# Building the token lists of a routed layer: number columns as 32-wide weights in four column groups, the one-hot table streamed, one small product to sum and turn

## The chip, the cores and the metric

The kernel runs on one core of one Trainium2 chip. The metric is the device time of one execution in microseconds (us), as the median of several runs; less is better. The core's engines are TensorE (PE; its weight loads are shown apart as PEld), VectorE (DVE), ScalarE (ACT), GpSimd (POOL), and SyncE (SP), which issues most DMAs. Each engine runs its own instructions strictly in the order in which the program gave them to it, and waits for the others by semaphores.

## The reference

Retention (attention with a decaying mask and no softmax) over 8 batches and 8 heads gives 4608 tokens of 512 numbers. They go through a layer of 8 experts with a fixed capacity of 576 tokens each, and through a dense two-layer network.

```python
scores = scale * np.matmul(q, k.transpose(0, 1, 3, 2))
ret = scores * Dmat[None, :, :, :]
x = np.matmul(ret, v)                       # 4608 x 512 after a reshape

logits = x @ w_gate                         # 4608 x 8
order = np.argsort(-logits.flatten())
for idx in order:                           # the greedy choice, with capacity 576
    tok, e = (int(idx) // E, int(idx) % E)
    if assigned[tok] >= 0 or counts[e] >= cap:
        continue
    assigned[tok] = e
    counts[e] += 1
for e in range(E):
    mask = assigned == e
    h = np.maximum(x[mask] @ w1[e], 0.0)
    out[mask] = h @ w2[e]

h = np.maximum(x @ w_in, 0.0)
return (h * h @ w_out).astype(np.float32)
```

## The kernel before

**Stages.** Attention runs for the first 169 us over 36 tiles of 128 tokens. Then `turn_back` writes the tokens to a DRAM table `xd` (36 groups of four PE transposes), while the router works out which 576 tokens the first expert gets. From about 218 us on, `moe(k)` for the experts k = 0 to 7 alternates with `mlp(j)`, the dense network on three tiles of 128 rows: one block after an even k, two after an odd k. An expert is two parts of 8 chunks f: a group of 12 products from `XH`, `XL` (the expert's tokens, turned) into a tile `mm` (L802), and, two chunks later, a group of 12 into the four `acc` tiles (L785). An `mlp` block is 16 chunks of a group of 12 (L865) and three groups of 9 (L849; one for each of its tiles).

**Weights.** `pump` moves the weight stream on: it splits one fetched chunk `raw` (two buffers, 512 KB) into a high and a low half `w` (ACT twice L628, POOL L629, DVE L630), and has SP fetch the next one into the buffer that came free. A chunk is split at most three ahead of use.

**Routing.** `Router.phase(k)` is a generator: it finds the threshold of expert k by binary search (`G`, `dg`, `cc`, `cx`, `cf`, `jk`; products L421 and L431), and then lists its tokens. At each `yield` it gives control back, and `slot()`, called twice in each chunk, moves it on by one step every few calls. `slot()` also moves on `load_tokens`, which waits until `listed(k)` has been called, issues the gathers of the expert's rows (POOL, L708, by the numbers in `idx`), and then `turn`s them: four PE transposes into `mm` (L716), ACT's copy `XH` (L724), DVE's difference `XL` (L725). When a part of `moe(k)` begins, `turned(n)` runs router and loader without pause until as many turns as the part needs (3, then 5) have been emitted.

**The list** of expert k (L498 to L518). DVE makes a one-hot table `OH` of 12 tokens tiles at a time, [128, 128, 12] f16 with the tile index t innermost, so that the 128 columns of one t lie 24 bytes apart. For each of 36 t, the PE loads the 128x128 slice `oh[:, :, t]` as weights and streams ten columns of `HC` (five of the token's tile number x 128, five of its row): all add into one `p[:, :10]`, which holds the numbers of the listed tokens already turned, one list entry to a partition. DVE copies `ids`, adds the two halves and writes `idx` as integers.

**The first expert's start** (L887 to L899): a loop moves the router and `turn_back` on and calls `pump` in each pass until the first list is done; then come 36 `warm` transposes, the loader until three turns are out, and one more `pump`.

Of the kernel before, what the change touches and what calls it, by code (L numbers as in the profile page):

```python
# [6 lines left out]
F32 = mybir.dt.float32  # L7
# [3 lines left out]
FH = mybir.dt.float16  # L11
# [4 lines left out]
NT = 36  # L16
# [53 lines left out]
def attention(tc, a, X, idn, rt, filler):  # L70

    nc = tc.nc
    L = rt.L
    with ExitStack() as c:
        cn = c.enter_context(tc.tile_pool(name="acn", bufs=1))
# [4 lines left out]
        def load(t, w0=0, w1=3):  # L80

            src = a["att"][t].rearrange("p (w g i) -> p w g i", w=3, g=4)
            if w0 == 0:
                T[t] = wk.tile([128, 2, 4, 128], F32, name="qk", bufs=5)
                nc.sync.dma_start(T[t], src[:, :2])
            if w1 == 3:
                V[t] = wk.tile([128, 4, 128], F32, name="v", bufs=4)
                nc.sync.dma_start(V[t], src[:, 2])
# [16 lines left out]
        wg = cn.tile([128, 4, 32], F32, name="wg")  # L105
        nc.vector.memset(wg, 0.0)
        nc.sync.dma_start(wg[:, :, :NE], a["wg"])
        nc.sync.dma_start(rt.f, a["rt"])
        load(3, 0, 2)
        load(2, 2, 3)  # L110
        load(4, 0, 2)
# [111 lines left out]
        for t in range(NT):  # L223
            if t + 2 < NT:
                turn_k(t + 2)
            if t + 1 < NT:
                weigh(t + 1)
                scores(t + 1)
            if t + 5 < NT:
                load(t + 5, 0, 2)  # L230
            if t + 3 < NT:
                load(t + 3, 2, 3)
            if t + 2 < 9:
                decay(t + 2)
            before(t)
            if t >= 4 and t % 2 == 0:
                next(todo, None)
            values(t)
            if t % 9 != 8:
                state(t)  # L240
            if t == NT - 2:
                ready = rt.prep(0, 32)
            if t >= NT - 2:
                next(ready)
            if t == 3:
                rt.start()
            next(filler, None)
        last = [gate(32, 35), gate(35, 36, "sp")]
        for g in last:
# [7 lines left out]
def route_tables():  # L257
    i = np.arange(128)
    tri = (i[:, None] < i[None, :]).astype(np.float32)
    u = np.zeros((128, 72), np.float32)  # L260
    j = np.arange(72)
    u[:72] = j[:, None] < j[None, :]
    thr = np.zeros((4, 16), np.float32)
    off = 0
    for r, step in enumerate(STEPS):
        thr[r] = np.arange(16) * step - off
        off += step
    sel = np.zeros((128, 4, 8), np.float32)
    for tl in range(4):
        sel[tl * 8:tl * 8 + 8, tl] = np.eye(8)  # L270
    f = np.concatenate([np.tile(thr.reshape(1, 64), (128, 1)),
                        np.tile(8.0 - np.arange(8), (128, 1)),
                        np.tile(128.0 * np.arange(36), (128, 1)),
                        i[:, None].astype(np.float32),
                        np.zeros((128, 8)),
                        np.tile(np.arange(8.0), (128, 1)),
                        np.tile(i, (128, 1)),
                        tri, u,
                        i[:, None] // 16 == np.arange(8),
                        i[:, None] % 16 == np.arange(16),  # L280
                        np.where(i < 8, CAP, BIG)[:, None],
                        sel.reshape(128, 32),
                        ], axis=1)
    return np.ascontiguousarray(f, np.float32)


# [6 lines left out]
class Router:  # L293
# [6 lines left out]
    def __init__(self, tc, pool):  # L300
        self.nc, self.ps = tc.nc, None
        t = pool.tile
        self.L = t([128, NT, 8], F32, name="L")
        f = self.f = t([128, 510], F32, name="rt")
        self.thr = f[:, 0:64].rearrange("p (r j) -> p r j", r=4)
        self.w8 = f[:, 64:72]
        self.t128 = f[:, 72:108]
        self.pcol = f[:, 108:109]
        self.e8 = f[:, 117:125]
        self.m8, self.m16 = f[:, 453:461], f[:, 461:477]  # L310
        self.c8 = f[:, 477:478]
        self.io = t([128, 128, 12], FH, name="io")
        self.b = t([128, 128 + 72], FH, name="rtb")
        self.tri, self.u = self.b[:, 0:128], self.b[:, 128:200]
        self.OH = [t([128, 128, 12], FH, name=f"OH{i}") for i in range(2)]
        self.sel = self.OH[0].rearrange("p s t -> p (s t)")[:, :512].rearrange("p (t m) -> p t m", t=4)
        self.ones = t([128, 128], FH, name="ones")
        self.U = t([128, NT], F32, name="U")
        self.AS = t([128, NT], F32, name="AS")
        self.C = t([128, 8], F32, name="C")  # L320
        self.idx = t([128, NT], I32, name="idx")
        self.es = t([1, NE], I32, name="es")
        self.A = t([128, NT + 12, 8], FH, name="A")
        self.V = t([128, NT, 8], F32, name="V")
        self.m = t([128, NT], F32, name="m")
        self.vm = t([128, NT], F32, name="vm")
        self.vu = t([128, NT], F32, name="vu")
        self.ki = t([128, 4, NT], I32, name="ki")
        self.kf = t([128, 2, NT], F32, name="kf")
        self.k2 = t([128, NT], F32, name="k2")  # L330
        self.B = t([128, 2], F32, name="B")
        self.G = t([128, NT + 4, 16], FH, name="G")
        self.c4 = t([128, 64], FH, name="c4")
        self.S8 = t([128, 16], FH, name="S8")
        self.dg = t([128, 8, 8], F32, name="dg")
        self.cc = t([128, 8], F32, name="cc")
        self.cx = t([128, 16, 8], FH, name="cx")
        self.cf = t([128, 16, 8], F32, name="cf")
        self.jm = t([128, 16], F32, name="jm")
        self.jk = t([128, 16], F32, name="jk")  # L340
        self.GT = t([128, 2, NT], F32, name="GT")
        self.NEW = t([128, 2, NT, 8], FH, name="NEW")
        self.wn = t([128, 16], FH, name="wn")
        self.nn = t([128, 48], F32, name="nn")
        self.DT = t([128, 2, NT], FH, name="DT")
        self.tot = t([72, 128], FH, name="tot")
        self.sl = t([128, 4, NT], F32, name="sl")
        self.si = t([128, 3, NT], I32, name="si")
        self.sb = t([128, 2, NT], FH, name="sb")
        self.h5 = t([128, NT, 5], FH, name="h5")  # L350
        self.HC = t([128, NT, 10], FH, name="HC")
        self.ids = t([128, 10], F32, name="ids")

    def start(self):
        v, f = self.nc.vector, self.f
        for x, c in ((self.sel, 0.0), (self.ones, 1.0), (self.U, 1.0), (self.AS, 0.0), (self.C, float(CAP)),
                     (self.A, 0.0), (self.G, 0.0)):
            v.memset(x, c)
        v.tensor_copy(self.io, f[:, 125:253].unsqueeze(2).to_broadcast([128, 128, 12]))
        v.tensor_copy(self.b, f[:, 253:453])  # L360
        v.tensor_copy(self.sel[:, :, 0:8], f[:, 478:510].rearrange("p (t e) -> p t e", t=4))

    def p(self):
        return self.ps.tile([128, 128], F32, name="rps")
# [75 lines left out]
    def phase(self, k):  # L440
        nc, v = self.nc, self.nc.vector
# [3 lines left out]
        if k < NE - 1:  # L445
# [7 lines left out]
            with nc.allow_low_precision("counts up to 36 are exact"):  # L453
                v.tensor_reduce(self.wn.rearrange("p (i e) -> p i e", i=2), self.NEW.rearrange("p i t e -> p i e t"),
                                axis=AX.X, op=OP.add)
            yield "long"
            yield
            p = self.p()
# [20 lines left out]
        p = self.p()  # L479
# [5 lines left out]
        p = self.p()  # L485
# [13 lines left out]
        p = self.p()  # L499
        for c in range(3):  # L500
            oh = self.OH[c % 2]
            v.tensor_tensor(oh, self.sb[:, 0, 12 * c:12 * c + 12].unsqueeze(1).to_broadcast([128, 128, 12]), self.io,
                            op=OP.is_equal)
            if c == 2:
                self.near(k)
            yield "long"
            for t in range(12):
                nc.tensor.matmul(p[:, :10], oh[:, :, t], self.HC[:, c * 12 + t, :],  # L508
                                 start=(c == 0 and t == 0), stop=(c == 2 and t == 11))
        v.tensor_copy(self.ids, p[:, :10])  # L510
        t0 = 9 * (k // 2)
        ia, ib = self.ids[:, 0:5], self.ids[:, 5:10]
        if k % 2 == 0:
            v.tensor_add(self.idx[:, t0:t0 + 4], ia[:, 0:4], ib[:, 0:4])
            v.tensor_add(self.idx[:64, t0 + 4:t0 + 5], ia[:64, 4:5], ib[:64, 4:5])
        else:
            v.tensor_add(self.idx[64:, t0 + 4:t0 + 5], ia[64:, 0:1], ib[64:, 0:1])
            v.tensor_add(self.idx[:, t0 + 5:t0 + 9], ia[:, 1:5], ib[:, 1:5])  # L518
        self.listed(k)
        if k < NE - 1:  # L520

# [63 lines left out]
def body(tc, a, out):  # L585
    nc = tc.nc
    with ExitStack() as ctx:
# [10 lines left out]
        with tc.tile_pool(name="cv", bufs=2) as cv:  # L598
            filler = convert(nc, a, cv, wd)
            attention(tc, a, X, idn, rt, filler)  # L600
            for _ in filler:
                pass
# [324 lines left out]
```

## Time and profile before

| | |
|---|---|
| time, median of 3 runs | 1531.27 us (1529.21 to 1531.87) |
| the profiled execution: time, span | 1525.86 us, 1524.1 us |
| busy share of the span: PE, PEld, DVE, ACT, POOL | 96%, 87%, 63%, 44%, 31% |
| list products and their weight loads, busy | 288 products, of 202 and 162 ns (medians) |
| chain of work that ended last, by engine | PE 73%, DVE 11%, DMA 6%, issue 5%, ACT 4% |

The span runs from the first instruction's start to the last one's end in the profiled execution; its own time is 1.76 us more, and 5.41 us (0.35%) under the median of the runs. An engine's busy share is a mean over stages that are limited by different things.

### The profile page before, as it was taken

The numbers are of one execution on the slowest core, as the hardware profiler recorded it, in microseconds if no ns is written. First come the engines' busy times: TensorE is split into PE (matmuls) and PEld (weight loads), VectorE is DVE, ScalarE is ACT, GpSimd is POOL, SyncE is SP. The second block draws the span as 40 slices with busy tenths as digits, with TensorE's granted clock in tenths as the row PEclk, the third lists the DMA queues.
The fourth block names the chain that finished last, engine by engine and source line by source line (L and its number), as shares of the span: only waits on it lengthen the run. The fifth ranks groups of instructions, "written<-read, shape, count | busy, mean of one in ns | idle before, by whom it ended". The sixth has DMA issues, their size and how long they took to land.

```text
span 1524.1 us, 27399 instructions
## 1 busy us (share of the span) xinstructions
PE 1462.2 (96%) x10599; PEld 1324.4 (87%) x10599; DVE 963.5 (63%) x1965; ACT 675.0 (44%) x1349; POOL 468.5 (31%) x410
## 2 busy tenths in 40 slices
PE   7998879999999999999999999999999999999997
PEld 6777768888988898889988899899888999999896
DVE  5999768766765657557765667567646455454341
ACT  6766644444433434334433344344334344444332
POOL 4454134544312224124213143233122431242110
PEclk9999979999999999999999999999999999999999
DMA  9999567224511224225313143234112351252110
GB/s 337 347 365 352 197 203 257 97 70 133 158 56 72 87 93 154 70 97 157 107 56 96 58 148 127 68 123 161 56 61 89 123 174 64 64 180 95 57 49 21
DMA packets 64210, 201.14 MB, mean 132 GB/s; under 512 B 8400, under 2 KB 8656, under 8 KB 64080
## 3 DMA queue, kind: packets, MB, share of 16 engines
q1 hardware_dynamic: 58128, 179.99, 35.2%
q0 software_dynamic: 5952, 19.40, 3.6%
q8 instruction: 83, 1.36, 0.4%
q14 instruction: 47, 0.39, 0.1%
HBM read 172.10 MB, written 27.26 MB: 131 GB/s over the span
## 4 chain that ended last, share of the span: by engine, by line
PE 73%; DVE 11%; DMA 6%; issue 5%; ACT 4%; POOL 0%; SPq 0%; ACTq 0%; DVEq 0%; POOLq 0%
PE mm L865 24%; PE acc L849 23%; PE acc L785 9%; PE mm L802 8%; DMA raw<-we 4%; DVE w L630 3%; PE px L205 2%; ACT w L628 1%; PE sc L165 1%; PE mm L716 1%; PE rps L508 1%; DVE cb L569 1%; DVE G L398 1%; DVE A L169 1%; DMA raw<-wd 1%
## 5 line engine op out<-in xcount | busy, mean ns | idle before, releaser
L629 POOL TENSOR_TENSOR w<-raw,w 128x512 fp32r<-128x512 f32 x212 | 278.0, 1311 | 825.8 <-ACT w L628 729.0
L630 DVE TENSOR_TENSOR w<-raw,w 128x512 fp32r<-128x512 f32 x212 | 265.4, 1252 | 228.7 <-ACT w L628 224.4
L628 ACT ACTIVATE w<-raw 128x512 fp32r<-128x512 f32 x424 | 243.3, 621 | 205.7 <-DMA raw<-we 163.0
L849 PE MATMUL acc<-big,h 128*128 128x512 f32 x972 | 246.0, 397 | 0.0
L785 PE MATMUL acc<-h,w 128*128 128x288 f32 x1536 | 224.4, 296 | 12.0 <-DVE YL L792 9.7
L785 PEld LDWEIGHTS acc<-h,w 128*128 128x128 f32 x1536 | 208.4, 188 | 14.6 <-DVE YL L792 11.6
L849 PEld LDWEIGHTS acc<-big,h 128*128 128x128 f32 x972 | 180.1, 188 | 35.4 <-DVE h L842 0.3
L871 ACT ACTIVATE r<-mm 128x384 f32<-128x384 f32 x192 | 93.9, 489 | 237.7 <-PE mm L865 217.2
L875 ACT ACTIVATE h<-r 128x384 fp32r<-128x384 f32 x192 | 100.9, 525 | 216.8 <-DVE r L873 216.8
L849 PE MATMUL acc<-w,h 128*128 128x512 f32 x756 | 190.9, 396 | 2.9 <-DVE h L842 2.9
L873 DVE TENSOR_TENSOR r<-mm,r 128x384 f32<-128x384 f32 x192 | 105.9, 551 | 125.5 <-ACT r L871 125.3
L865 PE MATMUL mm<-YH,big 128*128 128x384 f32 x864 | 173.4, 342 | 0.0
L849 PEld LDWEIGHTS acc<-w,h 128*128 128x128 f32 x756 | 139.3, 188 | 29.6 <-DVE h L842 3.7
L802 PE MATMUL mm<-XH,w 128*128 128x288 f32 x1024 | 161.0, 300 | 0.8 <-ACT XH L724 0.7
L865 PEld LDWEIGHTS mm<-YH,big 128*128 128x128 f32 x864 | 152.1, 188 | 7.7 <-ACT YH L791 0.9
L842 DVE TENSOR_TENSOR h<-r,h 128x384 fp32r<-128x384 f32 x192 | 110.9, 577 | 65.7 <-ACT h L875 65.7
L802 PEld LDWEIGHTS mm<-XH,w 128*128 128x128 f32 x1024 | 143.8, 190 | 2.0 <-ACT XH L724 1.1
L865 PE MATMUL mm<-YH,w 128*128 128x384 f32 x672 | 133.3, 339 | 0.0
L865 PEld LDWEIGHTS mm<-YH,w 128*128 128x128 f32 x672 | 117.6, 188 | 4.3
L865 PE MATMUL mm<-YL,big 128*128 128x384 f32 x432 | 93.4, 338 | 0.0
L802 PE MATMUL mm<-XL,w 128*128 128x288 f32 x512 | 89.0, 295 | 0.0
L865 PEld LDWEIGHTS mm<-YL,big 128*128 128x128 f32 x432 | 77.3, 188 | 0.3 <-DVE YL L792 0.2
(171 smaller groups left out, 1713.5 us busy)
## 6 DMA issues: line engine op xcount, KB each, us to landing
raw<-we SPq DMA_DIRECT2D x128, 512.0 KB, 3.6
raw<-wd SPq DMA_DIRECT2D x84, 512.0 KB, 3.2
qk<-att SPq DMA_DIRECT2D x36, 512.0 KB, 7.0
craw<-wm SPq DMA_DIRECT2D x32, 512.0 KB, 6.7
v<-att SPq DMA_DIRECT2D x36, 256.0 KB, 5.4
wd<-cb SPq DMA_DIRECT2D x32, 256.0 KB, 5.4
xd<-YH SPq DMA_DIRECT2D x18, 256.0 KB, 3.5
xd<-YL SPq DMA_DIRECT2D x18, 256.0 KB, 3.6
```

Source lines behind the costliest of these rows:

```text
L205: nc.tensor.matmul(px[o:o + 64, g, :], V[t][:, g, lo:lo + 64], D[t]["A"][i][:, g, :], start=(ph == 0), stop=True)
L628: nc.scalar.activation(w[:, 0], c, AF.Copy)
L629: nc.gpsimd.tensor_sub(w1[:, 1], raw[:, :512], w1[:, 0].bitcast(F32))
L630: nc.vector.tensor_sub(w2[:, 1], raw[:, 512:], w2[:, 0].bitcast(F32))
L785: nc.tensor.matmul(acc[part][d][:, :288], w2[:, wi, d * 128:(d + 1) * 128], h[:, xi, :288], start=(f == 0 and i == 0), stop=(f == 7 and i ...
L802: nc.tensor.matmul(p[:, :288], w1[:, wi, g * 128:(g + 1) * 128], X[xi][:, g, 288 * part:288 * part + 288], start=(g == 0 and i == 0), stop ...
L842: nc.vector.tensor_sub(h[:, 1], s, h[:, 0].bitcast(F32))
L849: nc.tensor.matmul(acc[t], h[:, xi, t * 128:(t + 1) * 128], w2[:, wi], start=(f == 0 and i == 0), stop=(f == 15 and i == 2))
L865: nc.tensor.matmul(p[:, :384], w1[:, wi, g * 128:(g + 1) * 128], Y[xi][:, g, o:o + 384], start=(g == 0 and i == 0), stop=(g == 3 and i == 2))
L871: nc.scalar.activation(r, p[:, :384], AF.Relu)
L873: nc.vector.tensor_mul(s, p[:, :384], r)
L875: nc.scalar.activation(h[:, 0], s, AF.Copy)
```

## The change

The roles of the two operands are swapped. `HC` grows from 10 to 32 columns (22 of them zero, set once by a memset) and becomes the weights; the one-hot slice is streamed, 128 columns. The product of t goes into the partitions 32 (t mod 4) and the 31 behind them of `p`, so four PE column groups each sum nine of the 36. DVE then copies the whole `p` to f16 (`lc`), the generator yields once more, and one product with `lc` as weights and five columns `s5` (ones that pick rows n and n+5 of each group) sums the groups and the two halves and turns the result. DVE writes `idx` straight from it. The table `rt` is cut into 150 columns that stay and 365 that only `start` reads.

```diff
-        nc.sync.dma_start(rt.f, a["rt"])
+        nc.sync.dma_start(rt.f, a["rt"][:, :150])
+        rf = cn.tile([128, 365], F32, name="rf")
+        nc.sync.dma_start(rf, a["rt"][:, 150:])
...
-                rt.start()
+                rt.start(rf)
...
-        self.HC = t([128, NT, 10], FH, name="HC")
-        self.ids = t([128, 10], F32, name="ids")
-
-    def start(self):
-        v, f = self.nc.vector, self.f
+        self.HC = t([128, NT, 32], FH, name="HC")
+        self.lc = t([128, 128], FH, name="lc")
+        self.s5 = t([128, 5], FH, name="s5")
+
+    def start(self, f):
+        v = self.nc.vector
         for x, c in ((self.sel, 0.0), (self.ones, 1.0), (self.U, 1.0), (self.AS, 0.0), (self.C, float(CAP)),
-                     (self.A, 0.0), (self.G, 0.0)):
+                     (self.A, 0.0), (self.G, 0.0), (self.HC, 0.0)):
             v.memset(x, c)
...
+        v.tensor_copy(self.s5, f[:, 360:365])
...
             yield "long"
             for t in range(12):
-                nc.tensor.matmul(p[:, :10], oh[:, :, t], self.HC[:, c * 12 + t, :],
-                                 start=(c == 0 and t == 0), stop=(c == 2 and t == 11))
-        v.tensor_copy(self.ids, p[:, :10])
+                r = slice(32 * (t % 4), 32 * (t % 4) + 32)
+                nc.tensor.matmul(p[r, :], self.HC[:, c * 12 + t, :], oh[:, :, t],
+                                 start=(c == 0 and t < 4), stop=(c == 2 and t > 7))
+        v.tensor_copy(self.lc, p)
+        yield
+        p = self.p()
+        nc.tensor.matmul(p[:, :5], self.lc, self.s5, start=True, stop=True)
         t0 = 9 * (k // 2)
-        ia, ib = self.ids[:, 0:5], self.ids[:, 5:10]
         if k % 2 == 0:
-            v.tensor_add(self.idx[:, t0:t0 + 4], ia[:, 0:4], ib[:, 0:4])
-            v.tensor_add(self.idx[:64, t0 + 4:t0 + 5], ia[:64, 4:5], ib[:64, 4:5])
+            v.tensor_copy(self.idx[:, t0:t0 + 4], p[:, 0:4])
+            v.tensor_copy(self.idx[:64, t0 + 4:t0 + 5], p[:64, 4:5])
         else:
-            v.tensor_add(self.idx[64:, t0 + 4:t0 + 5], ia[64:, 0:1], ib[64:, 0:1])
-            v.tensor_add(self.idx[:, t0 + 5:t0 + 9], ia[:, 1:5], ib[:, 1:5])
+            v.tensor_copy(self.idx[64:, t0 + 4:t0 + 5], p[64:, 0:1])
+            v.tensor_copy(self.idx[:, t0 + 5:t0 + 9], p[:, 1:5])
         self.listed(k)
```

The added `yield` also moves other instructions. Three places follow; rows give line, operation, tiles and shape, and the lines of the changed kernel are 9 higher here than those of before.

POOL, from the end of attention to the first expert; first before, then changed. `w` is the low half of a weight chunk, `xg` a gather of the first expert's tokens.

```order
L629 TENSOR_TENSOR w_3213<-raw,w_3213 128x512
L629 TENSOR_TENSOR w_3243<-raw,w_3243 128x512
L708 DMA xg<-xd,idx 128x512
L708 DMA xg<-xd,idx 64x512
L708 DMA xg<-xd,idx 128x512 x3
L629 TENSOR_TENSOR w_3319<-raw,w_3319 128x512
```

```order
L638 TENSOR_TENSOR w_3218<-raw,w_3218 128x512
L638 TENSOR_TENSOR w_3239<-raw,w_3239 128x512
L638 TENSOR_TENSOR w_3258<-raw,w_3258 128x512
L717 DMA xg<-xd,idx 128x512
L717 DMA xg<-xd,idx 64x512
L717 DMA xg<-xd,idx 128x512 x3
```

The loop at the first expert's start makes one pass more, and so calls `pump` once more: the third split stands ahead of the five gathers, where it stood behind them. On DVE and ACT the third split moves ahead of the first turns (`XL`, `XH`) likewise.

PE, from the last groups of the `mlp` block ahead of `moe(1)` to its first products; first before, then changed. `rps<-A,G` is a search step's product, `mm<-idn,xg` a turn. Of the ten rows of a step's five products with their weight loads, two are shown.

```order
L716 MATMUL mm<-idn,xg 128x128 x4
L849 MATMUL acc<-big,h 128x512 x9
...
L421 LDWEIGHTS G
L421 MATMUL rps<-A,G 128x64
L849 MATMUL acc<-w_4438,h 128x512 x9
L849 MATMUL acc<-big,h 128x512 x9
L802 MATMUL mm<-XH,w_4536 128x288 x8
```

```order
L725 MATMUL mm<-idn,xg 128x128 x4
L858 MATMUL acc<-big,h 128x512 x9
L858 MATMUL acc<-w_4445,h 128x512 x9
L858 MATMUL acc<-big,h 128x512 x9
...
L427 LDWEIGHTS G
L427 MATMUL rps<-A,G 128x64
L725 MATMUL mm<-idn,xg 128x128 x4
L811 MATMUL mm<-XH,w_4543 128x288 x8
```

All three turns that `moe(1)` needs stood among the chunks of the block; now the third stands behind its last group, directly ahead of the first product that reads it.

PE, the same place ahead of `moe(3)`; first before, then changed. `rps<-cx,ones` is the second half of a search step.

```order
L716 MATMUL mm<-idn,xg 128x128 x4
L849 MATMUL acc<-big,h 128x512 x9
...
L849 MATMUL acc<-w_7786,h 128x512 x9
L849 MATMUL acc<-big,h 128x512 x9
L802 MATMUL mm<-XH,w_7862 128x288 x8
```

```order
L858 MATMUL acc<-w_7784,h 128x512 x9
L858 MATMUL acc<-big,h 128x512 x9
L725 MATMUL mm<-idn,xg 128x128 x4
...
L427 LDWEIGHTS G
L427 MATMUL rps<-A,G 128x64
L437 LDWEIGHTS ones
L437 MATMUL rps<-cx,ones 128x128
L725 MATMUL mm<-idn,xg 128x128 x4
L811 MATMUL mm<-XH,w_7873 128x288 x8
```

Two of the three turns now stand behind the block's last group, with a whole search step (two products with DVE's work between them) squeezed in between them. Ahead of the other experts (k = 2, 4, 5, 6, 7) the turns move by a step or not at all and stay among the chunks.

## Rows read from the trace of the kernel before

**Rows 1.** Busy time by stretch: us, then engines (count), granted clock, DMA share, GB/s.

```profile
206.00:218.00 12.00, 7.74 (x49) 6.75 (x47) 4.84 (x15) 2.18 (x6) 6.81 (x7) 0.78 0.60 186
611.00:683.00 72.00, 72.00 (x399) 64.23 (x398) 41.33 (x97) 27.00 (x56) 14.16 (x13) 1.00 0.25 84
```

**Rows 2.** List products by line: duration ns min/median/max, first and last start.

```profile
L508 PEld LDWEIGHTS <-OH x288: 138/162/179, 203.1 to 1196.4; 128*128 128x128 f16 x144
L508 PE MATMUL rps<-HC,OH x288: 199/202/229, 203.1 to 1196.5; 128*128 128x10 f16 x144
```

**Rows 3.** Timeline, PE, in the first mlp block: start us, us, work, count.

```profile
316.51 2.25 PE L849 MATMUL acc<-w,h 128*128 128x512 f32 x9
318.60 0.89 PE L508 MATMUL rps<-HC,OH 128*128 128x10 f16 x12
319.35 1.65 PE L865 MATMUL mm<-YH,big 128*128 128x384 f32 x8
```

**Rows 4.** Products whose operands lie without gaps: by line, then on the timeline.

```profile
L421 PEld LDWEIGHTS <-G x240: 95/98/102, 227.9 to 1087.8; 128*128 128x128 f16 x120
679.02 0.32 PE L421 MATMUL rps<-A,G 128*128 128x64 f16 x5
```

**Rows 5.** Gate products in column groups of 32: timeline, with neighbour, then by line.

```profile
29.63 1.06 PE L127 MATMUL pr<-big,wg 128*32 128x512 f32 x8 [0.43 <-ACT kT L145]
30.63 1.09 PE L205 MATMUL px<-A,v 128*64 128x128 f32 x16
L127 PE MATMUL pr<-big,wg x72: 486/592/617, 29.6 to 169.1; 128*32 128x512 f32 x64, 128*32 128x384 f32 x8
```

**Rows 6.** Timeline at the first expert's start; last, the page's row of weight fetches.

```profile
205.40 1.36 DVE L630 TENSOR_TENSOR w<-raw,w 128x512 fp32r<-128x512 f32 x1 [0.47 <-DMA raw<-we]
208.19 1.13 POOL L708 DMA_INDIRECT xg<-xd,idx  x1 [0.30 <-DVE U L523]
211.93 0.66 PE L716 MATMUL mm<-idn,xg 128*128 128x128 f32 x4 [0.40 <-DMA xg<-xd,idx]
217.84 1.14 ACT L628 ACTIVATE w<-raw 128x512 fp32r<-128x512 f32 x2
218.00 2.29 PE L802 MATMUL mm<-XH,w 128*128 128x288 f32 x8 [0.69 <-ACT XH L724]
218.54 1.28 POOL L629 TENSOR_TENSOR w<-raw,w 128x512 fp32r<-128x512 f32 x1 [4.21 <-ACT w L628]
...
raw<-we SPq DMA_DIRECT2D x128, 512.0 KB, 3.6
```

**Rows 7.** The chain of waits in order of time, just after the first expert's start.

```profile
226.38 4.22 DMA raw<-we
```

**Rows 8.** Timeline where moe(1) begins.

```profile
357.49 2.00 ACT L853 ACTIVATE ot<-acc 128x512 f32<-128x512 f32 x3 [1.18 <-PE acc L849]
358.69 1.22 PE L802 MATMUL mm<-XH,w 128*128 128x288 f32 x8
```

**Rows 9.** Timeline where moe(3) begins.

```profile
680.89 0.22 DVE L424 TENSOR_TENSOR dg<-rps,rt 128x64 f32<-128x64 f32 x1
681.45 0.29 DVE L427 TENSOR_TENSOR cx<-cc,rt 128x128 f16<-128x128 f32 x1
683.43 1.21 PE L802 MATMUL mm<-XH,w 128*128 128x288 f32 x8
684.48 0.69 PE L802 MATMUL mm<-XL,w 128*128 128x288 f32 x4
685.64 0.60 ACT L724 ACTIVATE XH<-mm 128x512 fp32r<-128x512 f32 x1 [1.42 <-PE mm L716]
686.27 0.69 DVE L725 TENSOR_TENSOR XL<-mm,XH 128x512 fp32r<-128x512 f32 x1 [4.54 <-ACT XH L724]
687.25 0.28 DVE L432 TENSOR_TENSOR cf<-rps,C 128x128 f32<-128x128 f32 x1
688.15 1.02 DVE L398 SCALAR_TENSOR_TENSOR G<-kf,B,rt 128x448 f16<-128x448 f32 x2
```

More of the change, by code (lines that the diff above doesn't have):

```diff
@@ L282, in route_tables @@
                         sel.reshape(128, 32),
+                        (i[:, None] % 32 == np.arange(5)) | (i[:, None] % 32 == 5 + np.arange(5)),
                         ], axis=1)
+    f = np.concatenate([f[:, :125], f[:, 453:478], f[:, 125:453], f[:, 478:]], axis=1)
     return np.ascontiguousarray(f, np.float32)
@@ L303, in __init__ @@
         self.L = t([128, NT, 8], F32, name="L")
-        f = self.f = t([128, 510], F32, name="rt")
+        f = self.f = t([128, 150], F32, name="rt")
         self.thr = f[:, 0:64].rearrange("p (r j) -> p r j", r=4)
@@ L309, in __init__ @@
         self.e8 = f[:, 117:125]
-        self.m8, self.m16 = f[:, 453:461], f[:, 461:477]
-        self.c8 = f[:, 477:478]
+        self.m8, self.m16 = f[:, 125:133], f[:, 133:149]
+        self.c8 = f[:, 149:150]
         self.io = t([128, 128, 12], FH, name="io")
@@ L350, in __init__ @@
         self.h5 = t([128, NT, 5], FH, name="h5")
-        self.HC = t([128, NT, 10], FH, name="HC")
-        self.ids = t([128, 10], F32, name="ids")
-    def start(self):
-        v, f = self.nc.vector, self.f
+        self.HC = t([128, NT, 32], FH, name="HC")
[3 more added lines that the diff above has]
+        v = self.nc.vector
         for x, c in ((self.sel, 0.0), (self.ones, 1.0), (self.U, 1.0), (self.AS, 0.0), (self.C, float(CAP)),
-                     (self.A, 0.0), (self.G, 0.0)):
+                     (self.A, 0.0), (self.G, 0.0), (self.HC, 0.0)):
             v.memset(x, c)
-        v.tensor_copy(self.io, f[:, 125:253].unsqueeze(2).to_broadcast([128, 128, 12]))
-        v.tensor_copy(self.b, f[:, 253:453])
-        v.tensor_copy(self.sel[:, :, 0:8], f[:, 478:510].rearrange("p (t e) -> p t e", t=4))
+        v.tensor_copy(self.io, f[:, 0:128].unsqueeze(2).to_broadcast([128, 128, 12]))
+        v.tensor_copy(self.b, f[:, 128:328])
+        v.tensor_copy(self.s5, f[:, 360:365])
+        v.tensor_copy(self.sel[:, :, 0:8], f[:, 328:360].rearrange("p (t e) -> p t e", t=4))
     def p(self):
```

## The prediction

> **What bounds the kernel now.** I first read busy time by stretch, to see where PE time is the time. In the pair of `mlp` blocks ahead of `moe(3)` the PE is busy all 72.00 of 72.00 us [rows 1]: what a list product costs there is paid in full, and a stall there is new time. In the 12 us around the first expert's start it is busy 7.74 of 12, at a mean granted clock of 0.78 [rows 1]: there a chain of waits sets the pace. Then the list products by line: 288 products with as many weight loads, 199 to 229 ns and 138 to 179 ns [rows 2]. These durations overlap, so they are no price. The timeline gives one: a group of 12 starts at 318.60, the next group at 319.35 [rows 3]. A group costs the PE 0.75 us, 63 ns for each load and product.
>
> Of the 24 groups, the first three stand ahead of the first expert, behind DVE's tables; the other 21 stand among the `mlp` groups. Only these 21, 15.7 us together, are to be won from.
>
> **The list products.** A weight slice that lies without gaps loads in 98 ns (median) against 162 for a slice of the table [rows 4, 2], and five products with such slices take 0.32 us, of which some 0.20 us is the last one's own (a list product's 202 ns): (0.32 - 0.20)/4 = 30 ns a pair [rows 4, 2]. So the gaps cost the old group half its time. After the change `HC` (rows of 32 side by side) is loaded, and the table with its gaps is streamed, 128 columns where it was ten. What four column groups do is seen in the gate: eight f32 products of 32 weights by 512 columns, 592 ns each, span 1.06 us [rows 5]. One behind the other they would be 4.7 us, so four run side by side. The price of streaming with gaps is in no row. Bounds:
> - Low: reading costs nothing, and the products are issued at 30 ns a pair: 12 x 0.030 = 0.36 us. What follows changes the column mode: the group behind the gate starts only 0.06 us before the gate's modelled end, against 0.16 us for ordinary neighbours such as L849 and L508 [rows 5, 3]. That is about 0.1 us: 0.46 us a group, 21 x 0.29 = 6.1 us saved.
> - High: the gaps slow the stream as they slowed the load, and the groups share one read. The load lost 162 - 98 = 64 ns over 128 columns, so a column would take some 0.5 ns more; 128 x 0.9 = 115 ns a product, 12 in a row 1.4 us, with the mode 1.5 us: 21 x 0.75 = 15.8 us lost.
> - Taken: four side by side, three rounds, each at the gate's pace for f32 (1.06 us for two rounds of 512 columns is 0.13 us for 128), so that the gaps cost what f16 may win; with 0.1 us for the mode and 0.08 for the first loads, which cannot go ahead of it: 0.39 + 0.18 = 0.57 us, a saving of 0.18 us a group, **-3.8 us**. It is nearest to the gate's row, the only one with column groups.
>
> The row of the load says that gaps cost 64 ns for 128 columns. The Trainium skill ("SBUF — State Buffer", the note on cachelines under the port table) says that SBUF is read in 16-byte lines, needs at least two hits in a line for full bandwidth, and pays for each new line; columns 24 bytes apart hit a new line each. By the gate's row alone the sum stands at +6.8 us; by the page, with the load's 64 ns as the size of its penalty, near the high bound, at +26. No row here shows it for a streamed operand.
>
> **The small product and DVE.** One product more per list: a single search product squeezes between others for some 0.03 us; seven count, +0.3 us. DVE copies 128x128 instead of 128x10 and drops nothing big; it is not full in the `mlp` stretches (41.33 of 72 us) [rows 1]. A second table DMA, one memset and one copy in attention lie beside the PE there, at +0 to 0.7 us: **+0.3**.
>
> **The yield, first expert: +4.6 us.** Before, POOL splits two chunks and then gathers, at 208.19 [rows 6]. Now a third split stands ahead of the gathers on POOL, and of the first turns on ACT and DVE. POOL is in order, so the gathers wait for that chunk, though nothing in them needs it. Its fetch cannot leave before the first chunk's buffer is free: DVE's split ends at 205.40 + 1.36 = 206.76 [rows 6]. Fetches land after 3.6 us (median) [rows 6], 4.22 in this stretch's chain [rows 7]: about 210.8. ACT's first half ahead of POOL's split takes 218.54 - 217.84 = 0.70 us, the split 1.28 [rows 6]: POOL is free at 212.8, against 208.19. Behind the gathers wait the turns (first at 211.93) and the first product of `moe(0)` (218.00) [rows 6], all one chain, so +4.6 reaches 218. The chain behind it runs through the turns of the next tokens to a split and a fetch that its buffer releases (226.38) [rows 7]; that order is not changed, so the delay goes through. The third split comes out of the first chunk's way: up to 1.4 us back. A fetch on time at 3.5 us and 1.4 us back give +2.5; a fetch of 5 us and slower gathers +7.
>
> **The yield, moe(1): +0.9 us.** The third turn now stands last ahead of the first product of `moe(1)`. ACT has three copies `ot` that end at 357.49 + 2.00 = 359.49, 0.8 us behind the 358.69 where `moe(1)` began [rows 8]; then `XH` 0.60 [rows 9]. The first product starts 1.4 us later instead of 0.6 (the turn itself, which moved): +0.8 to 0.9, PE idle. Bounds 0.5 to 1.5.
>
> **The yield, moe(3): +4.5 us.** Two turns and a whole search step stand between the last group (its end E is 683.43) and the first product. ACT's `ot` copies end at about E+0.8 as above; `XH` to E+1.4, `XL` 0.69 to E+2.1 on DVE, ahead of the step's `dg`, `cc`, `cx`, which take 681.45 + 0.29 - 680.89 = 0.85 us, to E+3.0. Then the product, the third turn 0.6, `XH` 0.60: E+4.3. DVE meanwhile does `cf` to the end of the next `G`, 687.25 to 689.17 or 1.92 us, to E+5.2, and `XL` 0.69: E+5.9 [rows 9]. The first `XL` product came 1.05 us behind E [rows 9]. Of the 4.85 us between, about 1.0 are turns that only moved: 3.9 us lost. The clock fell after such thin work at the first expert's start [rows 1]; as much as 1.5 us more, 0.6 taken. Bounds 2 to 7. The other experts' turns stay among the chunks: nothing.
>
> **Sum.** -3.8 + 0.3 + 0.3 + 4.6 + 0.9 + 4.5 = **+6.8 us**, from 1525.86 to 1532.7 for a profiled execution. The median before is 5.41 us over the profiled one, so I set the sum on the median: 1531.27 + 6.8 = **1538.1 us**.
>
> **Rivals.**
> - *The stream with gaps is the bound* (the high price): 15.8 instead of -3.8, the sum +26.4, about 1558; with half the penalty 1548. For it: the load's 64 ns; against: the f32 gate feeds four groups at once. It decides from 0.75 us a group on.
> - *The stalls are covered*: the fetch is early, the gathers land faster because no weight fetch runs beside them, and at `moe(3)` the scheduler's copies clear sooner: +2.5, +0.5, +2 with the likely stream: -0.2, about 1531. For it: 1.4 us of splitting is taken out of the first chunk; against: in-order POOL with the fetch's 3.6 us.
> - *Faster*: the stream runs at the low price, 0.46 us a group, because issue and not reading paces it. The sum is then -6.1 + 0.6 plus the stalls. With them as taken (10.0), +4.5 (1535.8); it ends under before only if they are under 5.5 us together, half of what I have: at 2.5 + 0.5 + 2, -0.5 us; with the stalls nearly gone -5, 1526. The price it hangs on is the streaming of one group.
> - The Trainium skill ("TensorEngine Tiling (Array Packing)", Performance Considerations) recommends just this swap with four column groups where the streamed side is at most 32 wide; by it the low price would hold. Under Key Properties it says that a change of tiling mode drains the engine, which agrees with 0.06 against 0.16 us [rows 5, 3].
>
> **How the numbers follow.** 0.2% (3 us) is about what a measurement of this kernel can tell from no change. My forecast (stalls as worked out, stream between 0.46 and 0.65 us, +4 to +11): 0.50. Gaps as the bound (+12 to +27): 0.15. Stalls covered in part (-3 to +4): 0.23. Faster by more than 3 us: 0.12. Faster: 0.12. Within: 0.23 less a few at its upper end, 0.20. Slower: 0.68. The range leaves out the lowest tenth and the far half of the gap case: 1528.5 to 1550.
>
> **What would show it.** L515's groups: the next group's start 0.5 to 0.65 us behind theirs (right), 0.75 or more (gaps), 0.46 (low). POOL's first gather at about 212.8 with the third split ended just before it; the first product of `moe(0)` near 222.6. PE idle of about 0.9 us ahead of `moe(1)` and near 4 us ahead of `moe(3)`, released by `XH` and `XL`. I am wrong if the gathers start by 209, or if a list group falls or rises past these bounds.

## The result and the profile after

The changed kernel takes **1541.93 us** (median of 6 runs, 1538.16 to 1546.62) against 1530.88 before: a ratio of 1.0085, 95% interval 1.006 to 1.0109, so 9 to 17 us slower. The forecast was 1538.1, in 1528.5 to 1550. The profiled execution took 1543.86 us. The 23 runs of before beside the first four experiments (1526.49 to 1534.64) scatter by 8 us, and its first profile (1525.86) is below them all. A step between two single profiles can be off by 2.5 us (the last column of the table below), so verdicts rest on the ratios.

A group of list products on the timeline, columns as in [rows 3]:

```profile
336.73 2.25 PE L858 MATMUL acc<-w,h 128*128 128x512 f32 x9
338.91 0.86 PE L515 MATMUL rps<-OH,HC 128*32 128x128 f16 x12
339.71 1.67 PE L874 MATMUL mm<-YH,big 128*128 128x384 f32 x8
```

All of them by line, columns as in [rows 2]:

```profile
L515 PEld LDWEIGHTS <-HC x288: 92/97/128, 204.9 to 1224.8; 128*32 128x32 f16 x144
L515 PE MATMUL rps<-OH,HC x288: 383/406/427, 204.9 to 1225.0; 128*32 128x128 f16 x144
```

The weight loads fell from 162 to 97 ns, but the group holds the PE from 338.91 to 339.71, 0.80 us against 0.75 [rows 3] (medians of 21 groups 0.80 and 0.74). How it runs is seen by cutting this group into slices of 0.02 us; the number behind PE says how many products were at work in a slice, that behind PEld how many loads. The record of a product lasts about two rounds (406 ns), so eight are counted where four are still ending; the starts are what counts:

```profile
338.92:338.94 0.02, 0.02 (x4) 0.02 (x8) 1.00 0.00 0
339.10:339.12 0.02, 0.02 (x4) 0.00 (x0) 1.00 0.00 0
339.12:339.14 0.02, 0.02 (x8) 0.02 (x4) 1.00 0.00 0
339.32:339.34 0.02, 0.02 (x4) 0.00 (x0) 1.00 0.00 0
339.36:339.38 0.02, 0.02 (x8) 0.00 (x0) 1.00 0.00 0
339.56:339.58 0.02, 0.02 (x4) 0.00 (x0) 1.00 0.00 0
```

Four start at 338.91, four at 339.12, the last four at 339.34: the column groups do run side by side, but a round holds for 0.215 us, and 128 columns are then 1.7 ns each.

The first expert's start, columns as in [rows 6]:

```profile
207.58 1.34 DVE L639 TENSOR_TENSOR w<-raw,w 128x512 fp32r<-128x512 f32 x1 [0.84 <-DMA raw<-we]
210.60 0.14 DVE L524 CAST idx<-rps 64x1 int32<-64x1 f32 x1
212.51 1.15 ACT L637 ACTIVATE w<-raw 128x512 fp32r<-128x512 f32 x2 [3.77 <-DMA raw<-we]
213.22 1.28 POOL L638 TENSOR_TENSOR w<-raw,w 128x512 fp32r<-128x512 f32 x1 [3.17 <-ACT w L637]
214.66 1.39 POOL L717 DMA_INDIRECT xg<-xd,idx  x1 [0.16 <-DMA raw<-we]
223.81 2.29 PE L811 MATMUL mm<-XH,w 128*128 128x288 f32 x8 [0.69 <-ACT XH L733]
```

`idx` is ready at 210.74, and the first gather starts at 214.66, behind the third split, which waits for a chunk that could be fetched only when the first was split (208.92). Before, 0.22 us lay between `idx` (207.97) and the gather (208.19). Counted from the end of DVE's first split, the gather comes after 5.74 us, and before after 1.43 (208.19 - 206.76 [rows 6]).

The starts of `moe(1)` and of `moe(3)`, columns as in [rows 8]:

```profile
366.59 0.63 PE L725 MATMUL mm<-idn,xg 128*128 128x128 f32 x4
367.26 0.60 ACT L733 ACTIVATE XH<-mm 128x512 fp32r<-128x512 f32 x1
367.91 1.32 PE L811 MATMUL mm<-XH,w 128*128 128x288 f32 x8 [0.69 <-ACT XH L733]
...
694.49 0.69 DVE L734 TENSOR_TENSOR XL<-mm,XH 128x512 fp32r<-128x512 f32 x1 [2.47 <-ACT XH L733]
696.00 0.23 PE L437 MATMUL rps<-cx,ones 128*128 128x128 f16 x1 [2.08 <-DVE cx L433]
696.06 0.61 PE L725 MATMUL mm<-idn,xg 128*128 128x128 f32 x4
696.71 0.60 ACT L733 ACTIVATE XH<-mm 128x512 fp32r<-128x512 f32 x1 [2.25 <-PE mm L725]
697.36 2.28 PE L811 MATMUL mm<-XH,w 128*128 128x288 f32 x8 [0.69 <-ACT XH L733]
```

The first stretch of `moe(3)`, columns as in [rows 1]:

```profile
697.36:704.00 6.64, 6.64 (x43) 6.48 (x44) 4.06 (x9) 2.97 (x7) 1.31 (x2) 0.74 0.00 1
```

Ahead of `moe(1)` the PE idles 0.69 us for `XH`. Ahead of `moe(3)` it idles 2.08 for the squeezed search step and 0.69 for `XH`; then the granted clock falls, 0.74 on average over 6.64 us. Where 8 products take 1.21 us before [rows 9], they take 2.28.

Stage by stage, as the timelines give it (the time from the first product of a stage to the first of the next, less that of before's first profile, us):

| stretch | changed | yield alone | yield moved | moved, no third split | before again |
|---|---|---|---|---|---|
| start to `turn_back` | +1.85 | +1.38 | +2.45 | +1.74 | -1.17 |
| to the first product of `moe(0)` | +3.96 | +2.51 | +3.95 | +0.01 | -1.24 |
| `moe(0)` | +3.63 | +2.71 | +1.17 | +0.55 | +2.45 |
| `mlp` to the first product of `moe(1)` | -0.22 | -0.51 | +1.21 | +2.76 | -0.01 |
| the `mlp` block behind `moe(2)`, to that of `moe(3)` | +4.49 | +4.04 | +0.47 | +0.48 | -0.01 |
| `moe(3)` | +2.23 | +2.25 | +0.17 | +0.24 | -0.07 |

The last column is a second profile of the same kernel: attention and `moe(0)` differ by 1 to 2.5 us from one execution to the next, the later stretches of the table hardly at all (`moe(2)` and `moe(4)`, which it leaves out, by 1.5 and 1.1). The +2.76 holds a clock fall at 308 to 312 us.

### The profile page after: what moved, and what is told of

The parts are those of the page before. It is cut to its first block, busy times and chain, and to the rows that moved or that the text cites. A ratio compares the mean times of both kernels' runs of the same rounds, so it can differ in the third digit from the quotient of the medians.

```text
span 1542.1 us, 27414 instructions
## 1 busy us (share of the span) xinstructions
PE 1471.6 (95%) x10607; PEld 1318.7 (86%) x10607; DVE 962.6 (62%) x1967; ACT 677.0 (44%) x1349; POOL 468.1 (30%) x410
## 4 chain that ended last, share of the span: by engine, by line
PE 71%; DVE 11%; DMA 7%; issue 5%; ACT 4%; SPq 0%; POOL 0%; DVEq 0%; ACTq 0%; POOLq 0%
PE mm L874 24%; PE acc L858 24%; PE acc L794 8%; PE mm L811 7%; DMA raw<-we 5%; DVE w L639 3%; ACT w L637 1%; PE px L207 1%; PE mm L725 1%; PE sc L167 1%; PE rps L515 1%; DVE cb L578 1%; DVE G L404 1%; DVE A L171 1%; PE pr L145 1%
```

## The experiments

**The yield alone.** The kernel before with one line added:

```diff
         v.tensor_copy(self.ids, p[:, :10])
+        yield
```

> The kernel before, its list products and its table unchanged, with the one added yield (behind the copy of ids) and nothing else. Theory A (the added yield moves instructions, and the loss is what they wait for): 8 to 11 us slower than before, with a first gather some 4 us later, PE idle of about 1 us ahead of moe(1) and 4 us ahead of moe(3). Theory B (the new list products, the lc product and the table's work make the loss): within 2 us of before.

Measured: 1.0064 (1.0048 to 1.0081), +9.8 us. With the old products, the gathers start behind the third split here too; ahead of `moe(1)` the PE idles 0.69 us and ahead of `moe(3)` 2.08 and 0.69 (1 and 4 were expected), and the stretch up to `moe(3)` is 4.0 us longer, with a fall of the clock behind it. Theory A holds; the yield accounts for most of the loss.

**The yield moved.** The changed kernel with one step less elsewhere:

```diff
         v.tensor_mul(self.HC[:, :, 0:5], self.h5, self.t128.unsqueeze(2).to_broadcast([128, NT, 5]))
-        yield
```

> The changed kernel without the yield that stood between HC and the first one-hot table, so that a list takes as many steps as before; everything else of the change is in. Every expert but the first then starts as before; the third split still stands ahead of the first expert's gathers. Theory A: the part of moe(1) and moe(3) comes back, the first expert's start stays lost: 5 to 8 us slower than before, 4 to 6 faster than the changed kernel. Theory B: as slow as the changed kernel, 11 us over before.

Measured: 1.0051 (1.0032 to 1.007), +7.8 us, 5.2 under the changed kernel (the intervals leave 0.5 to 10). The stall ahead of `moe(3)` is gone (+0.47, of which three list groups at 0.06 us are 0.2) and `moe(3)` keeps its clock; the first expert's start is as late as in the changed kernel (+3.95).

**No third split either.** Further:

```diff
-            pump(0 not in near)
+            pump(0 not in near or st["split"] >= 2)
```

> As the kernel with the yield moved, and the loop ahead of the first expert splits no third chunk, so that POOL's order is that of before. Theory A: what is left is the list groups (0.79 against 0.75 us, 21 times: 0.9), the small products (0.3), attention (0.4) and DVE's second split ahead of idx (about 1): 1 to 4 us slower than before. Theory B: 8 us or more slower than before.

Measured: 1.0023 (1.0007 to 1.0039), +3.5 us. POOL on the timeline:

```profile
207.29 2.94 POOL L637 TENSOR_TENSOR w<-raw,w 128x512 fp32r<-128x512 f32 x2 [42.99 <-ACT w L636]
211.14 1.13 POOL L716 DMA_INDIRECT xg<-xd,idx  x1 [0.91 <-DVE U L531]
```

The first gather is released by DVE again, and the stretch ahead of `moe(0)` costs nothing (+0.01). The third split is worth 1.0051 - 1.0023 = 0.0028, 4.3 us (the intervals leave some 0.5 to 8). Taking that one step out of the list brings a wait of its own, in all five kernels that do so: the first list group in the first `mlp` block waits 1.1 to 1.2 us for ACT, where before the second one waits 0.50 us for its table.

```profile
319.57 0.87 PE L514 MATMUL rps<-OH,HC 128*32 128x128 f16 x12 [1.12 <-ACT r L879]
```

**The table without gaps.** The changed kernel, t first (the fill of `io` and the comparison change to match, not shown):

```diff
-        self.OH = [t([128, 128, 12], FH, name=f"OH{i}") for i in range(2)]
+        self.OH = [t([128, 12, 128], FH, name=f"OH{i}") for i in range(2)]
...
-                nc.tensor.matmul(p[r, :], self.HC[:, c * 12 + t, :], oh[:, :, t],
+                nc.tensor.matmul(p[r, :], self.HC[:, c * 12 + t, :], oh[:, t, :],
```

> The changed kernel with the one-hot table laid out t first, so that the 128 columns that a list product streams lie side by side. Theory C (the gaps set the pace of the stream, 0.215 us for a round of four): a round falls to 0.06 to 0.13 us and a group from 0.79 to 0.35 to 0.55 us, 5 to 9 us faster than the changed kernel unless DVE makes the table more slowly. Theory D (four column groups share one column at a time, whatever the layout): the group stays within 0.05 of 0.79 us.

Measured: 1.0032 (1.0017 to 1.0047), 8.1 us under the changed kernel. Two groups on its timeline:

```profile
335.67 0.35 PE L515 MATMUL rps<-OH,HC 128*32 128x128 f16 x12 [1.88 <-DVE OH L508]
...
340.32 0.35 PE L515 MATMUL rps<-OH,HC 128*32 128x128 f16 x12
340.60 1.67 PE L874 MATMUL mm<-YH,big 128*128 128x384 f32 x8
```

DVE's line that makes the table (duration ns min/median/max):

```profile
L508 DVE TENSOR_TENSOR OH<-sb,io x24: 1743/1750/2829, 203.5 to 1208.5; 128x1536 f16<-128x1536 f16 x24
```

0.28 us instead of 0.80: theory C, at less than the 0.35 to 0.55 expected. But DVE needs 1750 ns for a table instead of 950, now that the number that it compares with stands still along the innermost axis, and the PE waits for it up to 1.88 us among the `mlp` groups.

**One column group.** The changed kernel, all 36 products into partitions 0 to 31, `lc` and `s5` cut to 32 rows:

```diff
-                r = slice(32 * (t % 4), 32 * (t % 4) + 32)
-                nc.tensor.matmul(p[r, :], self.HC[:, c * 12 + t, :], oh[:, :, t],
+                nc.tensor.matmul(p[:32, :], self.HC[:, c * 12 + t, :], oh[:, :, t],
```

> The changed kernel with all 36 list products in one column group (partitions 0 to 31), the table as it was. If the four groups share one read of 0.42 ns a column, the group of 12 stays near 0.8 us; if each group reads its own columns at 1.7 ns, four side by side, it rises to about 2.7 us.

A group on its timeline:

```profile
334.33 2.88 PE L514 MATMUL rps<-OH,HC 128*32 128x128 f16 x12
337.14 1.66 PE L873 MATMUL mm<-YH,w 128*128 128x384 f32 x8
```

2.81 us a group (the one execution: 1592.38 us), 0.23 a product. A stream with gaps takes as long alone (0.23 us) as with three others (0.215 a round); four groups are worth a factor of 3.5, and they do not slow one another.

**Pairs, without the moves.** The kernel without moves, the table in pairs of t. DVE still writes, reads and compares runs of two:

```diff
-        self.OH = [t([128, 128, 12], FH, name=f"OH{i}") for i in range(2)]
+        self.OH = [t([128, 6, 128, 2], FH, name=f"OH{i}") for i in range(2)]
...
-            v.tensor_tensor(oh, self.sb[:, 0, 12 * c:12 * c + 12].unsqueeze(1).to_broadcast([128, 128, 12]), self.io,
+            v.tensor_tensor(oh, self.sb[:, 0, 12 * c:12 * c + 12].rearrange("p (a b) -> p a b", b=2).unsqueeze(2).to_broadcast([128, 6, 128, 2]), self.io,
...
-                nc.tensor.matmul(p[r, :], self.HC[:, c * 12 + t, :], oh[:, :, t],
+                nc.tensor.matmul(p[r, :], self.HC[:, c * 12 + t, :], oh[:, t // 2, :, t % 2],
```

> The kernel with the yield moved and no third split, with the one-hot table laid out in pairs of t: the columns that a list product streams lie 4 bytes apart instead of 24, and DVE still writes runs of two f16. Theory C (a column in a 16-byte line of its own sets the pace): the group falls from 0.79 to 0.28 to 0.35 us as in the table without gaps, and with DVE's table at 0.95 to 1.1 us the time is 8 to 10 us under the kernel it is made from, some 5 us under before. Theory D2 (any gap costs the same): the group stays at 0.79 us, the time at 3 us over before.

A group on its timeline, and then DVE's line that makes the table:

```profile
318.60 0.36 PE L514 MATMUL rps<-OH,HC 128*32 128x128 f16 x12
318.88 1.66 PE L873 MATMUL mm<-YH,big 128*128 128x384 f32 x8
```

```profile
L507 DVE TENSOR_TENSOR OH<-sb,io x24: 945/952/955, 203.1 to 1175.6; 128x1536 f16<-128x1536 f16 x24
```

Measured: **0.9944 (0.9923 to 0.9965), 1521.10 us**, 8.6 us under before and 12 under the kernel it is made from; 21 groups at 0.52 us less are 10.9 of it. DVE's table keeps its 952 ns. This version beats both kernels.

**Before, with pairs.** The same table in the kernel before, its operands not swapped:

```diff
-                nc.tensor.matmul(p[:, :10], oh[:, :, t], self.HC[:, c * 12 + t, :],
+                nc.tensor.matmul(p[:, :10], oh[:, t // 2, :, t % 2], self.HC[:, c * 12 + t, :],
```

> The kernel before, its list products as they were, with the table in pairs of t: the weight slices' columns lie 4 bytes apart instead of 24. Theory C: the load falls from 162 towards 98 ns and the group from 0.75 to 0.4 to 0.5 us, 21 times: 5 to 7 us faster than before, without the swap of operands. Theory D2: no difference that can be measured.

A group on its timeline, and then its weight loads by line:

```profile
329.10 0.46 PE L508 MATMUL rps<-HC,OH 128*128 128x10 f16 x12
329.41 1.65 PE L865 MATMUL mm<-YH,big 128*128 128x384 f32 x8
```

```profile
L508 PEld LDWEIGHTS <-OH x288: 96/97/117, 203.8 to 1188.8; 128*128 128x128 f16 x144
```

Measured: 0.9945 (0.9928 to 0.9962), 8.4 us faster. The weight load fell from 162 to 97 ns and the group from 0.74 to 0.32 us (medians): 21 x 0.43 = 9.0, more than the 5 to 7 expected. With pairs the swap is worth 0.03 us a group (0.31 and 0.28 in the lines shown), and the two kernels' times do not differ (0.9945 and 0.9944).

**The changed kernel with pairs, its moves kept.** Nothing but the table differs from the changed kernel:

```diff
-        self.OH = [t([128, 128, 12], FH, name=f"OH{i}") for i in range(2)]
+        self.OH = [t([128, 6, 128, 2], FH, name=f"OH{i}") for i in range(2)]
```

> The changed kernel, its yield and its third split as they are, with the table in pairs of t and nothing else. If layout and moves add up (layout worth 12 us between the two kernels without moves), it comes out 11 to 13 us under the changed kernel, 0 to 3 us of before; if the time won in the list groups only fills waits that the moves leave, it stays 5 us or more over before.

Measured: 1.0007 (0.9993 to 1.002), no difference from before, 12 us under the changed kernel. Layout and moves add up: pairs are worth 0.0078 with the moves and 0.0079 without, the moves 0.0062 with gaps and 0.0063 with pairs (9.5 us). Each of the four is good to about 0.003, so that they agree this closely is in part luck.

**Fours and sixes**, the kernel in pairs without moves, with 4 and 6 in place of 2:

```diff
-        self.OH = [t([128, 6, 128, 2], FH, name=f"OH{i}") for i in range(2)]
+        self.OH = [t([128, 3, 128, 4], FH, name=f"OH{i}") for i in range(2)]
```

> The kernel in pairs without moves, in fours: columns 8 bytes apart, so two in every 16 bytes. By the Trainium skill's rule (two hits in a line give full bandwidth) a group takes 0.28 us as with pairs; if the pace falls with every byte of distance it lies between 0.28 and 0.80, at some 0.36 to 0.45 us.

> The same in sixes: columns 12 bytes apart, so that two of three steps go to another 16 bytes. By the line rule a group is slower than with pairs, between 0.4 and 0.8 us; if only distances of 16 bytes and more cost, it stays at 0.28 us.

A group on the timeline of each, fours first:

```profile
327.60 0.52 PE L514 MATMUL rps<-OH,HC 128*32 128x128 f16 x12
328.05 1.67 PE L873 MATMUL mm<-YH,big 128*128 128x384 f32 x8
```

```profile
316.21 0.70 PE L514 MATMUL rps<-OH,HC 128*32 128x128 f16 x12
316.83 1.66 PE L873 MATMUL mm<-YH,big 128*128 128x384 f32 x8
```

Over 21 groups the medians are 0.45 and 0.62 us (one execution each, 1532.61 and 1524.88 us, too few to set against one another). The price rises with the distance between columns: 0.28 us at 2 and at 4 bytes, 0.45 at 8, 0.62 at 12, 0.80 at 24. It does not rise in step with the bytes: from 8 to 12 it adds 0.18, and from 12 to 24 another 0.18. (At 12 bytes three of four steps, not two of three, go to another 16 bytes.)

**Before again**, unchanged, for a second profile:

> The kernel before, unchanged, for a second profile. Its first profile (1525.86 us) is under all its timed runs, and the profiles of four other kernels show clock falls near 150, 264 and 597 us that it does not. Theory E (such falls are chance of one execution): this profile shows some of them too and lies nearer to 1531 us. Theory F (they come from the edits, the extra yield or the new products): it shows none of them.

1528.11 us; a clock fall at 590 to 594 us, none near 150 or 264. The fall near 595 is chance, as theory E has it. That near 150 stands also in the kernel with the yield alone, whose attention is that of before, so no edit makes it; I count it as chance too. That near 264 comes behind a wait of the PE for `YL`, and the length of the wait does not decide: here 3.26 us left the granted clock at 1.00, and in the kernel with the yield moved 1.75 us were followed by 0.50. First this kernel, then that; the second line of each is the stretch behind, columns as in [rows 1]:

```profile
257.71 1.85 PE L785 MATMUL acc<-h,w 128*128 128x288 f32 x12 [3.26 <-DVE YL L792]
257.71:262.00 4.29, 4.29 (x35) 4.14 (x36) 3.87 (x11) 1.04 (x2) 0.70 (x1) 1.00 0.32 92
```

```profile
264.11 2.72 PE L793 MATMUL acc<-h,w 128*128 128x288 f32 x12 [1.75 <-DVE YL L800]
264.80:268.20 3.40, 3.40 (x19) 3.25 (x19) 2.79 (x7) 0.63 (x1) 0.91 (x1) 0.50 0.24 41
```

## Why the prediction was right or wrong

**Direction and range: right.** The sum was +6.8 us; measured +13 by the ratio (9 to 17), +11 by the medians. That is at or past the upper end of the +4 to +11 that had half of the chance; the range reached further because it held half of the gap case.

**The stalls: right in place and in sum; of their three terms one was too large and one too small.** Ten of the forecast's microseconds were the yield's (4.6 + 0.9 + 4.5); the yield alone measures 9.8, the moves in the two pairs of kernels that differ only by them 9.5. One by one:

- The first expert's start: +4.6 forecast. The first gather comes 4.3 us later behind the first split (5.74 against 1.43), and 4.3 us (0.5 to 8) lie between the kernels with and without the third split.
- `moe(1)`: 0.9 forecast, 0.69 idle, and nothing lost: the stretch up to it is 0.2 us shorter than before. Near the end of the same block the PE before waits 1.45 us for `h`. That wait (1.45 to 1.48 us) stands in all eight profiles with the third turn among the chunks and in none of the five with it behind the last group, so the move took away about as much as it cost. The prediction had not seen it:

```profile
354.75 1.90 PE L849 MATMUL acc<-w,h 128*128 128x512 f32 x7 [1.45 <-DVE h L842]
```

- `moe(3)`: 4.5 forecast, 3.9 for the chain and 0.6 for the clock. The stretch ahead is 4.5 us longer, 2.8 of it idle in the two waits, and `moe(3)` itself 2.2: together 6.7, and 6.3 with the yield alone. The clock's share is larger than the 0.6 taken: 3.4 us at half the clock (an estimate of 1.7 lost). The clock falls within 1.5 us of the start of `moe(3)` in four of the five profiles with this order of instructions (all but that with one column group), in none of the eight with the turns among the chunks.

So the 10.0 met 9.8 in part by luck: by the profiles the terms are about 4.3, 0 and 6.5. `moe(1)` and `moe(3)` together were 5.4 in the forecast and are 1.0085 - 1.0051 = 0.0034, or 5.2 us (0.5 to 10), in the times.

**The list groups: the step that failed.** "Taken: four side by side, three rounds, each at the gate's pace for f32 (...) so that the gaps cost what f16 may win": a round was taken at 0.13 us and measured 0.215, the group at 0.57 and measured 0.80. So the term of -3.8 us is +1.0 (21 x 0.05; 1.3 by the medians 0.80 and 0.74). By its own sign, 0.75 us or more, the rival of the gaps as the bound held, at +1.0 us and not at its +15.8. The f32 gate was the nearest row, but its columns lie side by side, and its pace says nothing of gaps. The row that spoke of them, 162 against 98 ns for a weight load [rows 2, 4], was kept for the high bound only, and there wrongly joined with a shared read: one column group alone at 0.23 us a product shows that the four do not slow one another. Nor had it the size: its 115 ns a product in three rounds gives 0.35 + 0.18 = 0.53 us a group. No row before priced a streamed column 24 bytes from the next; it measured 1.7 ns. With +1.0 in its place the sum is +11.6, or 1542.9 us. Two slips leave the forecast as it is: the rival of the covered stalls adds up to +1.8 (-3.8 + 0.6 + 5.0), about 1533, and not to -0.2; and the 72.00 us of [rows 1] are one `mlp` block, not a pair.

**The Trainium skill's rule that was weighed** ("SBUF — State Buffer", the note on cachelines) pointed the right way: the gaps are what undid the swap. Its sentence that two hits in a 16-byte line give full bandwidth is not borne out: two columns in every 16 bytes cost 0.45 us a group against 0.28 for four. Counted in such lines, the 128 columns of a product touch 64 at 8 bytes, 96 at 12 and 128 at 24, and the group rises by the same 0.18 us each time: the three fit a price for each line touched, which no run tested further. And its recipe of swap and column tiling ("TensorEngine Tiling (Array Packing)", Performance Considerations) is worth 0.31 against 0.28 us a group here once the columns lie 4 bytes apart in both.

**The small product, DVE and attention: not settled.** +0.6 was forecast; the kernel without moves is 3.5 us over before (1.1 to 6.0), of which 1.0 are the groups. The rest is not resolved from zero. In that profile the PE waits 1.8 us for `lc` at the first expert, DVE's second split stands ahead of `idx`, and the first list group waits 1.12 us for ACT; none was tried alone. Likewise `moe(0)` is 3.6 us longer in the changed kernel's profile, with a clock fall behind a wait of 3.91 us for `YL`; but before's second profile has 2.45 of it, without a fall. Against before's first profile the six with the third split lie at -1.1 to +3.6 us there, the six others at -2.6 to +2.4, so how much of it is the change stays open.

## What to carry to other kernels

When a product's operands are swapped, the gaps in the layout go from the load to the stream: ask first for the layout, which here was worth 8 us with the table loaded as weights and 12 with the table streamed, and keep pairs of f16 together so that VectorE's write stays as fast. A `yield` in a step that is woven into other work is an edit of the order of every engine: count what it pushes behind a wait on an in-order queue, and also which waits it takes away. Price a stream by a row with the same distance between elements, or measure that distance by itself.

## What the runs showed of the hardware that was not expected

- TensorE streams f16 columns 4 bytes apart as fast as without gaps (0.28 us a group of 12); at 8, 12 and 24 bytes the group takes 0.45, 0.62 and 0.80. Four column groups side by side each read with gaps at the pace of one alone (0.215 us a round, 0.23 a product alone).
- VectorE compares and writes [128, 1536] f16 in about 950 ns with runs of 2, 4, 6 or 12 elements lying together in all operands, and in 1750 when one operand stands still along the innermost axis.
- The PE idled 2.08 and 0.69 us with 0.61 us of turns between at the start of `moe(3)`, and the clock fell from 2.4 to 1.2 GHz: for 3.4 us of full work in the changed kernel and with the yield alone, for 6.8 in two other profiles, and not at all with one column group. After a single idle gap it can go either way: 3.26 us left it at 2.4, 1.75 us were followed by 1.2.
